# Selecting the 32nd maximum from the larger and the smaller ones of column pairs

## Chip, cores and metric

One core of a Trainium2 chip runs the whole program. The metric is the device time of one execution in microseconds; for the kernel before it is the median of three runs. A profile of one execution of the kernel before is used throughout.

Engines are called as in the profile: PE multiplies matrices (PEld is its loading of weights), DVE, ACT and POOL work on vectors, SP issues most DMAs.

## What is computed

Top-k attention is followed by a Fourier mixing block. The attention part has batch 8, 8 heads, 576 tokens and 64 channels a head:

```python
scores = scale * np.matmul(q, k.transpose(0, 1, 3, 2))
kth = np.partition(scores, -top_k, axis=-1)[..., -top_k:-top_k + 1]   # top_k = 32
mask = scores >= kth
scores = np.where(mask, scores, -1000000000.0)
scores = scores - np.max(scores, axis=-1, keepdims=True)
attn = np.exp(scores)
attn = attn / (np.sum(attn, axis=-1, keepdims=True) + 1e-09)
return np.matmul(attn, v).astype(np.float32)
```

So each of the 8 x 8 x 576 rows of 576 scores needs its largest and its 32nd largest value. The heads are then joined to x of 576 x 512 per batch, and the second block takes the real part of a two-dimensional Fourier transform over tokens and channels, adds x, normalises each row, and applies a two-layer network (512 to 2048 to 512, with a ReLU between) whose output is added again.

## The kernel before, in words

**Items and steps.** Two heads of a batch form a pair; there are 32 pairs, four to a batch. Each pair gives nine items of 128 rows by 576 scores (the ninth joins the tails of both heads), 288 items in all. The main loop (lines 1542 to 1684) makes one step per item, and in step i it works on several items at once: PE makes the scores of item i+3, DVE selects in items i and i+1, ACT and POOL mask item i-1, ACT takes its exponential, and items further back are transposed and multiplied with v.

**Selection.** `top_ops` (line 428) makes DVE's instructions for one item. There are four rounds. In each, a MAX8 (line 446) finds the eight largest values of each row into eight columns of the tile m, and except in the last a MATCH_REPLACE8 (line 448) copies the row to the work tile wk with those eight replaced by a very small number. The profile shows a MATCH_REPLACE8 as two instructions, a MATCH_VALUE_LOAD of the eight values and the pass itself. All seven passes run over 576 columns. Rounds 0 and 1 of item i+1 and rounds 2 and 3 of item i are issued alternately in one step (lines 1657 to 1663), so that neighbours on DVE do not depend on each other; the plan's "shift" operation, if the step has one, comes behind the last of item i.

**After the selection.** `bounds` (line 451) is a POOL instruction (line 455, tile nt) that multiplies columns 0 and 31 of m, the largest and the 32nd largest value, by constants from cc. `mask` (line 466) has ACT write 0 or a very large number to wk (line 469), and POOL subtract that from the scores (line 472). `expo` (line 476) is ACT's exponential with the sum of the row (line 480). For most pairs `plane` (line 487) splits the result into two planes of 16 bits (line 493), SP writes them to memory (line 506), and `turn` (line 515) brings them back transposed; `attend` (line 576) multiplies with v on PE.

**What runs beside it.** In batch 0, the first 36 steps, no network work is ready yet, and the weights are prepared instead: each of 32 pieces takes a shift on DVE (line 217) and two operations on POOL (lines 236 and 238), with ACT conversions between. POOL also subtracts column means from the first weights (line 1410). From batch 1 on, PE does the network of the batch before (lines 1024, 1051, 1218) in between. Units of it are handed to steps by an estimate of PE's time (`fixed_cost`, `level` and the "room" of a step); those estimates are constants written in the code and know nothing of DVE or POOL. POOL adds up folds of the Fourier transform (lines 684, 695, 760; DVE does them for the first and last batch) and sums for the network (lines 1164, 1191).

**Order.** The order on each engine is that in which the code issues. Within a step, POOL's queue has the mask of the item before, planned operations ("pool0"), `some_sums`, `bounds`, more sums, then the rest of the plan. SP's queue has the DMAs in the same order.

**Buffers.** The tile m has five buffers of 32 columns; the scores S six; the work tiles W three for pairs of items and one for the joined tails.

Of the kernel before, what the change touches and what calls it, by code (L numbers as in the profile page):

```python
# [9 lines left out]
F32 = mybir.dt.float32  # L10
I32 = mybir.dt.int32
# [3 lines left out]
ALU = mybir.AluOpType  # L15

TOPK = 32
NEG = -3.4028234e38
FAR = 2.0 ** 100
P = 128  # L20
# [66 lines left out]
def kernel(  # L87
# [7 lines left out]
    out: bass.AP,  # L95
):
    nc = tc.nc
    B, H, S, D = q.shape
    DM = H * D
    DF = moe_w_ch1.shape[1]  # L100
    scale = 1.0 / float(D) ** 0.5
    HS = S // 2
# [18 lines left out]
    fs_np, fd_np, sg_np, turn_np, rows_np = _tables(S, DM)  # L121
    fs_d = nc.inline_tensor(fs_np, name="c_fs")
    fd_d = nc.inline_tensor(fd_np, name="c_fd")
    sg_d = nc.inline_tensor(sg_np, name="c_sg")
    turn_d = nc.inline_tensor(turn_np, name="c_turn")
    rows_d = nc.inline_tensor(rows_np, name="c_rows")
# [4 lines left out]
    small = ctx.enter_context(tc.tile_pool(name="small", bufs=4))  # L131
# [30 lines left out]
    cc = const.tile([P, 2], F32, name="cc", tag="cc")  # L162
# [80 lines left out]
    nat, qT_of, kT_of, v_of, PT, Ssb, Wk, Wp, M8, Nt = ({} for _ in range(10))  # L243
# [109 lines left out]
    N = len(items)  # L353
# [71 lines left out]
            nc.scalar.copy(out=s_t[r, keys], in_=sp[r])  # L425
        return 1.04

    def top_ops(i, rounds):

        if not 0 <= i < N:  # L430
            return []
# [12 lines left out]
        for r in rounds:  # L444
            src, m8 = s if r == 0 else w, m[:, 8 * r:8 * r + 8]
            ops.append(lambda src=src, m8=m8: nc.vector.max(out=m8, in_=src))  # L446
            if r < TOPK // 8 - 1:
                ops.append(lambda src=src, m8=m8: nc.vector.match_replace(w, m8, src, NEG))  # L448
        return ops

    def bounds(i):

        if i < N:
            Nt[i] = small.tile([P, 2], F32, name=f"nt_{i}", tag="nt", bufs=6)
            nc.gpsimd.tensor_tensor(  # L455
                out=Nt[i], in0=M8.pop(i)[:, 0:TOPK:TOPK - 1], in1=cc, op=ALU.mult
            )

    def pair_by_dma(pair):

        return NPB <= pair < NPAIR - 1 and pair != 2 * NPB - 1
# [860 lines left out]

    ctx.enter_context(tc.manual_schedule())
    nc.vector.memset(cc[:, 0:1], -1.0)

    warm = small.tile([P, 1], F32, name="warm", tag="rd", bufs=6)
    kn0 = batp.tile([P, NC, 2, D], F32, name="kn0", tag="y")
# [113 lines left out]
    for b in range(B):  # L1441
        end = PER_BATCH * (b + 1) - 1
        last = b == B - 1
        first, soon = b == 0, b == 1
# [28 lines left out]
        for n, t in enumerate((0, 1, 4)):  # L1473
            s = fc + (0 if quick else n // 2)
            at(s, "pe2", lambda b=b, t=t, q=quick: dft_channels(b, t, q), 1.75)
        for n, t in enumerate((0, 1, 4, 3, 2)):
            s = fc + (n // 3 if last else 0 if first else (0, 0, 1, 1, 2)[n])
# [58 lines left out]
            got += one_unit()  # L1536
        return got

    for op in top_ops(0, (0, 1)):
        op()  # L1540
    i, carry = 0, 0.0
    while i < N + 5 or plan or queue or sums:
# [53 lines left out]
        if short:  # L1596
            fixed += tok
            pair, r = divmod(i - 1, PER_PAIR)
# [12 lines left out]
        cost, got = carry, 0.0  # L1611
# [36 lines left out]
        if i < N:  # L1648
# [72 lines left out]
```

## Time and profile before

| what | value |
|---|---|
| three runs | 1788.68, 1789.32, 1792.17 us |
| median | 1789.32 us |
| profiled execution | 1791.8 us |
| its span, first to last instruction | 1790.0 us |
| mean granted PE clock | 0.961 |
| busy PE / DVE / ACT / POOL | 1641.4 / 1538.2 / 1277.7 / 927.3 us |
| MAX8, 1152 instructions | 743 to 747 ns each |
| MATCH_REPLACE8, 864 instructions | 740 ns each |
| POOL's mask subtraction (line 472), 288 | 1415 ns each |
| POOL's bounds (line 455), 288 | 204 ns each |

An engine's busy time counts its own instructions, so an engine that is busy nearly all of a stretch sets that stretch's length unless another one is just as full. Which one it is changes over the run, so the stages have to be read apart. Instructions of one engine overlap a little at their ends; the distance from one start to the next tells what an instruction costs its engine.

### The profile page before, as it was taken

How to read it: one execution, taken by the hardware profiler on the slowest of the kernel's cores; microseconds unless marked ns; L12 is line 12 of the kernel's file. 1: busy time of each engine (PE TensorE's matmuls, PEld its weight loads, DVE VectorE, ACT ScalarE, POOL GpSimd, SP SyncE). 2: the span in 40 equal slices, each digit the busy share in tenths (PEclk: the TensorE clock that was granted, in tenths of full speed). 3: DMA queues.
4: the chain of work that ended last, by engine and by line, in shares of the span. 5: the costliest groups of instructions: out<-in, count | busy, mean ns of one | idle time of the engine just before them, and what ended most of it. 6: DMA issues, size and time to landing. Idle time of an engine off the chain costs nothing.

```text
span 1790.0 us, 26146 instructions
## 1 busy us (share of the span) xinstructions
PE 1641.4 (92%) x7782; PEld 1036.8 (58%) x7782; DVE 1538.2 (86%) x3284; ACT 1277.7 (71%) x3132; POOL 927.3 (52%) x1284
## 2 busy tenths in 40 slices
PE   5666688999889999999999999999999999999998
PEld 3444455455455654557555765566565755576677
DVE  7999989998899999999999999999999999861110
ACT  6878748777788778877787778877887778652200
POOL 4768845655644565355553665356535555343122
PEclk7877799999999999999999999999999999999999
DMA  5333115751457855577556865596557755630051
GB/s 155 114 102 114 34 34 149 214 155 44 121 132 199 214 145 131 141 210 193 129 148 179 222 138 138 148 240 151 141 139 212 189 134 140 169 90 13 6 180 59
DMA packets 486589, 248.97 MB, mean 139 GB/s; under 512 B 364336, under 2 KB 476720, under 8 KB 486448
## 3 DMA queue, kind: packets, MB, share of 16 engines
q1 hardware_dynamic: 482672, 237.51, 50.6%
q0 software_dynamic: 2816, 9.44, 1.5%
q8 instruction: 62, 1.02, 0.2%
q14 instruction: 79, 0.65, 0.1%
q10 hardware_dynamic: 960, 0.36, 0.1%
HBM read 93.49 MB, written 84.74 MB: 100 GB/s over the span
## 4 chain that ended last, share of the span: by engine, by line
PE 52%; DVE 14%; ACT 14%; POOL 13%; issue 5%; DMA 2%; SPq 1%; POOLq 0%; DVEq 0%
PE hp L1024 19%; DVE m L446 6%; PE o L585 6%; DVE wk L448 6%; POOL wk L472 4%; PE cp L1051 4%; PE cw L1218 4%; PE cv L1218 4%; PE sp L422 4%; ACT wk L469 3%; POOL fold L695 3%; PE cp L1089 2%; ACT wk L493 2%; ACT S L480 2%; PE yp L782 2%
## 5 line engine op out<-in xcount | busy, mean ns | idle before, releaser
L472 POOL TENSOR_TENSOR wk<-S,wk 128x576 f32<-128x576 f32 x288 | 407.6, 1415 | 445.1 <-ACT wk L469 437.7
L446 DVE MAX8 m<-wk 128x8 f32<-128x576 f32 x864 | 618.8, 743 | 0.1
L1024 PE MATMUL hp<-unT,w 128*128 128x256 f32 (+1 forms) x2048 | 527.3, 408 | 8.2 <-ACT hT L1028 6.8
L1024 PEld LDWEIGHTS hp<-unT,w 128*128 128x128 f32 x2048 | 378.0, 191 | 112.0 <-ACT hT L1028 11.7
L448 DVE MATCH_REPLACE8 wk<-m,wk 128x576 f32<-128x576 f32 x576 | 426.3, 740 | 0.0
L469 ACT ACTIVATE wk<-S,nt 128x576 f32<-128x576 f32 x288 | 224.4, 779 | 93.5 <-POOL nt L455 93.0
L493 ACT COPY wk<-S 128x576 uint16<-128x576 uint16 x468 | 290.5, 674 | 0.0
L1051 PE MATMUL cp<-w,hT 128*128 128x512 f32 x512 | 236.3, 600 | 0.0
L446 DVE MAX8 m<-S 128x8 f32<-128x576 f32 x288 | 215.1, 747 | 12.5 <-ACT S L396 12.3
L480 ACT ACTIVATE S<-wk,nt 128x576 f32<-128x576 f32 x234 | 185.1, 791 | 46.6 <-POOL wk L472 45.3
L585 PE MATMUL o<-PT,v 128*64 128x256 f32 (+3 forms) x1440 | 199.5, 422 | 15.4 <-ACT x L648 5.2
L448 DVE MATCH_REPLACE8 wk<-m,S 128x576 f32<-128x576 f32 x288 | 213.2, 740 | 0.0
L1028 ACT ACTIVATE hT<-hp 128x320 f32<-128x320 f32 (+1 forms) x256 | 104.0, 414 | 152.3 <-PE hp L1024 150.1
L422 PE MATMUL sp<-kT,qT 64*128 64x512 f32 (+1 forms) x528 | 163.8, 665 | 10.2 <-ACT means L1414 5.7
L585 PEld LDWEIGHTS o<-PT,v 128*64 128x64 f32 x1440 | 115.6, 155 | 94.3 <-issue 26.5
L425 ACT COPY S<-sp 128x512 f32<-128x512 f32 (+1 forms) x264 | 142.1, 589 | 30.3 <-PE sp L422 29.7
L1051 PEld LDWEIGHTS cp<-w,hT 128*128 128x128 f32 x512 | 93.4, 194 | 88.1 <-issue 86.9
L455 POOL TENSOR_TENSOR nt<-m,cc 128x2 f32<-128x2 f32 x288 | 58.9, 204 | 155.0 <-DVE m L446 151.7
L1164 POOL TENSOR_TENSOR hT<-hT 128x512 f32<-128x512 f32 x64 | 81.2, 1274 | 78.3 <-ACT hT L1028 55.0
L1218 PE MATMUL cw<-w,hT 128*128 128x256 f32 x448 | 106.1, 387 | 8.2 <-ACT ct L1189 4.2
L392 PEld LDWEIGHTS sp_t<-kt,qT 128*128 128x128 f32 x320 | 51.3, 194 | 104.2 <-issue 72.6
L1218 PEld LDWEIGHTS cw<-w,hT 128*128 128x128 f32 x448 | 84.1, 193 | 24.2 <-ACT ct L1189 6.2
(151 smaller groups left out, 2039.8 us busy)
## 6 DMA issues: line engine op xcount, KB each, us to landing
planes<-wk SPq DMA_DIRECT2D x208, 288.0 KB, 2.7
w<-w_parts SPq DMA_DIRECT2D x82, 512.0 KB, 5.3
space<-in_moe_w_ch_dram SPq DMA_DIRECT2D x32, 512.0 KB, 3.4
nat<-in_q_dram SPq DMA_DIRECT2D x128, 64.0 KB, 2.3
v<-in_v_dram SPq DMA_DIRECT2D x32, 256.0 KB, 3.2
nat<-in_k_dram SPq DMA_DIRECT2D x62, 128.0 KB, 3.4
planes<-wk SPq DMA_DIRECT2D x52, 144.0 KB, 2.6
w_parts<-w_t POOLq DMA_DIRECT2D x8, 512.0 KB, 4.2
```

The lines of the kernel that those rows point to most:

```text
L422: nc.tensor.matmul(sp[r], lhsT=qT[hd, q_cols], rhs=kT[hd, :], start=True, stop=True)
L425: nc.scalar.copy(out=s_t[r, keys], in_=sp[r])
L446: ops.append(lambda src=src, m8=m8: nc.vector.max(out=m8, in_=src))
L448: ops.append(lambda src=src, m8=m8: nc.vector.match_replace(w, m8, src, NEG))
L469: nc.scalar.activation(out=w, in_=Ssb[i], func=AF.Relu, scale=-FAR, bias=Nt[i][:, 1:2])
L472: nc.gpsimd.tensor_tensor(out=w, in0=Ssb[i], in1=w, op=ALU.subtract)
L480: nc.scalar.activation(out=Ssb[i] if by_dma(i) else w, in_=w, func=AF.Exp, bias=Nt.pop(i)[:, 0:1], accum_out=den_t[pair % 3][:, c:c + 1],)
L493: nc.scalar.copy(out=words[:, half, :], in_=src[:, half, :])
L585: nc.tensor.matmul(o[D * e:D * (e + 1), c0:c1], lhsT=vv[:, e, c, :], rhs=pt[:, NF if c == NF else (NF + 1) * e + c, c0:c1], start=(c == 0) ...
L1024: nc.tensor.matmul(hp[:, 0:w], lhsT=w1[:, dt, P * it:P * (it + 1)], rhs=unT[:, dt, 0:w], start=(dt == 0), stop=(dt == NDT - 1),)
L1051: nc.tensor.matmul(cp, lhsT=hT[:, it, P * n:P * (n + 1)], rhs=w2[:, it, :], start=(it == 0), stop=(it == NIT - 1),)
L1218: nc.tensor.matmul(dst, lhsT=h()[a][:, kc, :], rhs=rhs_of(kc), start=start and kc == 0, stop=kc == NK - 1, skip_group_check=True,)
```

## The change

The 576 columns of an item are taken as 288 pairs: column c and column c + 288. DVE writes the larger one of each pair to the first half of the work tile ("won") and the smaller one to the second half ("lost"). The four rounds of MAX8 and the three of MATCH_REPLACE8 then run over the 288 larger ones and give their 32 largest. One MAX8 over the 288 smaller ones gives their eight largest. A scan over eight columns, `meet`, joins the two ordered lists: its state starts with the 32nd winner and becomes, in turn, the minimum of the next higher winner and the maximum of the state and the next loser. Its last value is the 32nd largest of all 576, as long as no more than eight losers belong there.

That condition is checked. After the bounds of each item, a second POOL instruction keeps, in one column `beaten`, the largest difference so far between the 8th loser and the 24th winner. After the last item DVE turns it into ones and zeros, PE counts the rows over which it is positive, DVE writes the count as an integer, and at the end of the program every engine reads it. If it is above zero, the whole program runs once more with the selection as before. The body is therefore a function `forward` that is built twice, the second time inside a condition.

In a step the split for the larger ones comes first for item i+1; the split for the smaller ones comes behind the first MAX8 of item i's second part, the MAX8 of the smaller ones before the last MAX8, and `meet` behind it. The tile m has 48 columns and three buffers, not 32 and five, and `bounds` takes columns 0 and 47.

```diff
+    beaten = pool.tile([P, 1], F32, name="beaten", tag="beaten")
+    again = pool.tile([1, 1], I32, name="again", tag="again")
+    args = (tc, q, k, v, moe_w_ch1, moe_w_ch2, out, tables, beaten, again)
+    forward(*args, True)
+    rows = nc.values_load(again, min_val=0, max_val=P)
+    with tc.If(rows > 0):
+        forward(*args, False)
...
-            M8[i] = small.tile([P, TOPK], F32, name=f"m8_{i}", tag="m8", bufs=5)
-        w, m, s = Wk[i], M8[i], Ssb[i]
-        ops = []
-        for r in rounds:
-            src, m8 = s if r == 0 else w, m[:, 8 * r:8 * r + 8]
-            ops.append(lambda src=src, m8=m8: nc.vector.max(out=m8, in_=src))
-            if r < TOPK // 8 - 1:
-                ops.append(lambda src=src, m8=m8: nc.vector.match_replace(w, m8, src, NEG))
+            M8[i] = small.tile([P, KTH + 1], F32, name=f"m8_{i}", tag="m8", bufs=3)
+        return Wk[i], M8[i], Ssb[i]
...
+    LOST, MET, KTH = TOPK, TOPK + 8, TOPK + 15
...
+        w, m, s = work(i)
+        won, lost = (w[:, 0:HS], w[:, HS:S]) if in_pairs else (w, None)
+
+        def split(to, op):
+            return lambda: nc.vector.tensor_tensor(
+                out=to, in0=s[:, 0:HS], in1=s[:, HS:S], op=op
+            )
+
+        def best(r):
+            src = won if r or in_pairs else s
+            return lambda: nc.vector.max(out=m[:, 8 * r:8 * r + 8], in_=src)
+
+        def strike(r):
+            src = won if r or in_pairs else s
+            return lambda: nc.vector.match_replace(won, m[:, 8 * r:8 * r + 8], src, NEG)
+
+        def meet():
+
+            nc.vector.tensor_tensor_scan(
+                out=m[:, MET:MET + 8], data0=m[:, LOST:LOST + 8],
+                data1=m[:, TOPK - 2:TOPK - 10:-1], initial=m[:, TOPK - 1:TOPK],
+                op0=ALU.max, op1=ALU.min,
+            )
+
+        if part == 0:
+            ops = [split(won, ALU.max)] if in_pairs else []
+            return ops + [best(0), strike(0), best(1), strike(1)]
+        ops = [best(2), strike(2), best(3)]
+        if in_pairs:
+            ops[1:1] = [split(lost, ALU.min)]
+            ops[3:3] = [lambda: nc.vector.max(out=m[:, LOST:LOST + 8], in_=lost)]
+            ops.append(meet)
         return ops
...
+            last = KTH if in_pairs else TOPK - 1
+            m = M8.pop(i)
             nc.gpsimd.tensor_tensor(
-                out=Nt[i], in0=M8.pop(i)[:, 0:TOPK:TOPK - 1], in1=cc, op=ALU.mult
-            )
+                out=Nt[i], in0=m[:, 0:last + 1:last], in1=cc, op=ALU.mult
+            )
+            if in_pairs:
+                nc.gpsimd.tensor_scalar(
+                    out=beaten, in0=m[:, LOST + 7:LOST + 8],
+                    scalar1=m[:, TOPK - 9:TOPK - 8], scalar2=beaten,
+                    op0=ALU.subtract, op1=ALU.max,
+                )
...
+    def count_rows():
+
+        got = bank([1, 1], "rows")
+        nc.tensor.matmul(got, lhsT=beaten, rhs=cc[:, 0:1], start=True, stop=True)
+        nc.vector.tensor_scalar(
+            out=again, in0=got, scalar1=-1.0, scalar2=None, op0=ALU.mult
+        )
+        return 0.2
+
+    if in_pairs:
+        at(N + 1, "dve", lambda: nc.vector.tensor_scalar(
+            out=beaten, in0=beaten, scalar1=0.0, scalar2=None, op0=ALU.is_gt
+        ))
+        at(N + 4, "pe", count_rows)
...
-        first, second = top_ops(i, (2, 3)), top_ops(i + 1, (0, 1))
+        first, second = top_ops(i, 1), top_ops(i + 1, 0)
```

More of the change, by code (lines that the diff above doesn't have):

```diff
@@ L97, with forward @@
     nc = tc.nc
+    S, DM = q.shape[2], q.shape[1] * q.shape[3]
+    tables = tuple(
+        nc.inline_tensor(t, name=n)
+        for t, n in zip(_tables(S, DM), ("c_fs", "c_fd", "c_sg", "c_turn", "c_rows"))
+    )
+    pool = ctx.enter_context(tc.tile_pool(name="found", bufs=1))
+    beaten = pool.tile([P, 1], F32, name="beaten", tag="beaten")
[5 more added lines that the diff above has]
+        forward(*args, False)
+@with_exitstack
+def forward(
+    ctx, tc, q, k, v, moe_w_ch1, moe_w_ch2, out, tables, beaten, again, in_pairs
+):
+    nc = tc.nc
+    fs_d, fd_d, sg_d, turn_d, rows_d = tables
     B, H, S, D = q.shape
@@ L119 @@
     ROWS = {0: P, 1: P, 2: P, 3: P, 4: TAIL}
[L121 to L126, printed above, removed]
     const = ctx.enter_context(tc.tile_pool(name="const", bufs=1))
@@ L426, in scores, with work @@
         return 1.04
-    def top_ops(i, rounds):
-        if not 0 <= i < N:
-            return []
+    def work(i):
         if i not in Wk:
@@ L440, in top_ops @@
             Wk[i] = Wp[i - 1][:, 1, :] if e == 1 else Wp[i][:, 0, :]
-            M8[i] = small.tile([P, TOPK], F32, name=f"m8_{i}", tag="m8", bufs=5)
-        w, m, s = Wk[i], M8[i], Ssb[i]
-        ops = []
-        for r in rounds:
-            src, m8 = s if r == 0 else w, m[:, 8 * r:8 * r + 8]
-            ops.append(lambda src=src, m8=m8: nc.vector.max(out=m8, in_=src))
-            if r < TOPK // 8 - 1:
-                ops.append(lambda src=src, m8=m8: nc.vector.match_replace(w, m8, src, NEG))
+            M8[i] = small.tile([P, KTH + 1], F32, name=f"m8_{i}", tag="m8", bufs=3)
+        return Wk[i], M8[i], Ssb[i]
+    LOST, MET, KTH = TOPK, TOPK + 8, TOPK + 15
+    def top_ops(i, part):
+        if not 0 <= i < N:
+            return []
+        w, m, s = work(i)
[24 more added lines that the diff above has]
+            ops.append(meet)
         return ops
@@ L1324 @@
     nc.vector.memset(cc[:, 0:1], -1.0)
+    if in_pairs:
+        nc.vector.memset(beaten, -1.0)
     warm = small.tile([P, 1], F32, name="warm", tag="rd", bufs=6)
@@ L1537, in some @@
         return got
-    for op in top_ops(0, (0, 1)):
+    def count_rows():
[5 more added lines that the diff above has]
+        return 0.2
+    if in_pairs:
+        at(N + 1, "dve", lambda: nc.vector.tensor_scalar(
+            out=beaten, in0=beaten, scalar1=0.0, scalar2=None, op0=ALU.is_gt
+        ))
+        at(N + 4, "pe", count_rows)
+    for op in top_ops(0, 0):
         op()
```

## The prediction, made before the change was built

> **What bounds the kernel now.** I read the page's busy table and slices first. PE is busy 92% of the span, DVE 86%; DVE shows 9 in nearly every slice up to the 35th, PE only from the eighth. So two engines are near full, in different stretches. I then asked for the busy time of each engine in six stretches cut where that picture changes (columns: stretch, length, busy us of PE, PEld, DVE, ACT, POOL, granted clock, DMA share, GB/s):
>
> ```profile
> 0.00:230.00 230.00, 147.70 (x726) 90.33 (x727) 216.58 (x454) 179.87 (x420) 164.40 (x177) 0.78 0.33 101
> 230.00:315.00 85.00, 76.61 (x345) 47.03 (x344) 78.15 (x173) 59.56 (x154) 37.24 (x56) 0.94 0.38 97
> 315.00:540.00 225.00, 201.85 (x919) 115.71 (x918) 204.32 (x434) 172.24 (x439) 125.90 (x187) 0.95 0.50 135
> 540.00:765.00 225.00, 212.53 (x1002) 131.52 (x1000) 219.75 (x469) 179.84 (x439) 114.15 (x165) 0.98 0.64 165
> 765.00:1575.00 810.00, 794.31 (x3846) 497.89 (x3847) 766.18 (x1639) 638.07 (x1553) 429.94 (x623) 1.00 0.65 168
> 1575.00:1790.00 215.00, 208.41 (x952) 154.30 (x949) 53.23 (x120) 48.15 (x129) 55.63 (x80) 1.00 0.20 65
> ```
>
> The first 230 us (batch 0, about 38 items) belong to DVE: 94% busy with PE at 64%, and the chain of waits there gives 41% to lines 446 and 448. From 540 to 765 DVE (98%) leads, PE loses 12.5 us. From 765 to 1575 PE is at 98%: 150 items, 5.4 us each, and only 16 us of PE are idle. The last 215 us are PE alone. A faster selection can win much only at the start; later it is capped by PE's idle time, 23 + 12.5 + 16 us.
>
> Next, the costs: the groups of instructions, and the DVE timeline of one plain step.
>
> ```profile
> L446 DVE MAX8 m<-wk 128x8 f32<-128x576 f32 x864 | 618.8, 743 | 0.1
> L448 DVE MATCH_REPLACE8 wk<-m,wk 128x576 f32<-128x576 f32 x576 | 426.3, 740 | 0.0
> ```
> ```profile
> 67.51 0.40 DVE L217 TENSOR_SCALAR w<-w 128x512 int32<-128x512 int32 x1
> 67.84 0.07 DVE L448 MATCH_VALUE_LOAD wk<-m,wk 128x8 f32 x1
> 67.91 0.73 DVE L448 MATCH_REPLACE8 wk<-m,wk 128x576 f32<-128x576 f32 x1
> 68.57 0.74 DVE L446 MAX8 m<-S 128x8 f32<-128x576 f32 x1
> 69.23 0.73 DVE L446 MAX8 m<-wk 128x8 f32<-128x576 f32 x1
> ...
> 72.67 0.40 DVE L217 TENSOR_SCALAR w<-w 128x512 int32<-128x512 int32 x1
> ```
>
> Durations overlap; what counts is the distance of starts. A MAX8 or a MATCH_REPLACE8 takes 0.66 us of the engine, a MATCH_VALUE_LOAD 0.065. An item costs 7 x 0.663 + 3 x 0.065 = 4.84 us; with the shift (0.33) that makes 5.17, and the step above is 72.67 - 67.51 = 5.16.
>
> **The selection after the change.** No row has MAX8 on 288 columns. TENSOR_TENSOR rows give the rate: 128x256 takes 427 ns and 128x510 690, so 1.035 ns a column. Taking 288 columns (0.298) off leaves 0.365 us. The bounds are 0.33 (half of 0.663) and 0.66 (no gain); I take 0.365, as the fixed part must stay. Five MAX8 and three MATCH_REPLACE8: 8 x 0.365 = 2.92. Three loads: 0.20. The two splits are TENSOR_TENSORs of 288 columns; line 684 starts 0.34 us apart at 256 columns, so 0.373 each, 0.75. The scan of 8 has no row: below it lies the 0.06 us of a MATCH_VALUE_LOAD, above it the 0.42 of a 256-column op; I take 0.25, a RECIPROCAL of six columns (0.18) and 0.07 for waiting on the MAX8 right ahead. Sum 4.12: **0.72 us less per item** if nothing interferes.
>
> **What interferes.** The splits read two operands from SBUF, and POOL is busy half of the time. DVE hardly does such ops now, but where it does, batch 0's folds, this is the timeline of both engines:
>
> ```profile
> 227.64 0.43 DVE L684 TENSOR_TENSOR near<-x 128x256 f32<-128x256 f32 x1
> 227.69 0.82 POOL L695 TENSOR_TENSOR ftail<-fold 64x63 f32<-64x63 f32 x2
> 227.98 2.33 DVE L684 TENSOR_TENSOR far<-x 128x256 f32<-128x256 f32 x1
> 228.46 0.18 POOL L698 COPY ftail<-fold 64x1 f32<-64x1 f32 x1
> 228.58 0.09 POOL L725 MEMSET ftail<- 64x1 f32 x1
> 228.64 1.40 POOL L472 TENSOR_TENSOR wk<-S,wk 128x576 f32<-128x576 f32 x1
> ```
>
> The same op takes 0.43 and then 2.33 us, ending 0.27 after POOL's mask subtraction. The other such op (at 1639.8) took 1.49 and ended 0.28 after POOL's; line 217, one input, spreads from 397 to 1494 ns in the same way. So a split that finds POOL at work waits for POOL's op and then needs some 0.15 us less than its full time. How long is that wait? At a random moment the rest of POOL's running op is on average the sum of d x d / 2 over its ops, divided by the stretch. A weight step of batch 0 (5.42 us) has ops of 1.29, 1.42 and 1.34 us: 5.48 / 2 / 5.42 = 0.5; over all POOL ops of the timeline I count 0.45 for 0:230, 0.28 for 540:765, 0.29 for 765:1575. Less 0.15 in the share of moments when POOL works (0.71 and 0.5), a split pays 0.35 in batch 0 and 0.21 later. Two splits: 0.70 and 0.42. The bounds are nothing (always between POOL's ops) and 1.9 each (the row above). **The net gain per item is then 0.0 in batch 0 and 0.3 later.**
>
> The Trainium skill (SBUF — State Buffer, "Who interferes with whom") says that a DVE instruction with two SBUF inputs contends with a GpSimd instruction that reads SBUF, and that the second to issue blocks until the first is done. By that rule one op is waited for at most, up to 1.27 us for a split beside the mask; the 2.33 row let several ops of POOL pass, so it is worse than the rule.
>
> **POOL** gets 288 more ops of one column (line 455's two-column rows: 0.20 us; bounds 0.18 and 0.39) and is itself held by splits. In a plain weight step it idles 0.87 us of 5.16, which covers 0.2 + 0.5. Where batch 0's 16 mean subtractions (line 1410, 1.28 us) are added nothing covers it: 16 x 0.4 = 6 us. The op stands behind line 455 and before the mask subtraction, which waits some 1.5 us for ACT (437.7 us over 288), so it delays nothing else there.
>
> **Buffers of m** go from 5 to 3: the first MAX8 of item i+1 now waits for POOL's bounds of i-2. In the timeline these would be late in 12 steps, 19 us together, all after 315 where POOL's folds make it lag up to 11 us. PE leads there, so I count 3 us; bounds 0 and 19. The split writes the work tile 1.3 us earlier than the first MATCH_REPLACE8 did; DVE waits for copies out of that tile 4.7 us in all now, so nothing, or some 3 us if that grows. Nt's operand now waits for the scan, but the following MATCH_REPLACE8 no longer lies behind it: nothing.
>
> **The end.** Matmul and two DVE ops of the count lie beside the last batch's 180 us of PE: nothing (0.5 if not). The read of the count on every engine and the jump come after the last store. No row has either; below 0.02 us (a semaphore event), above 15 (about four round trips). I take two round trips at the 3.96 us of the first load from memory: 8 us. The Trainium skill (Runtime: NRT & Kernel Launch, "Instruction fetch mechanics") says that a jump outside the fetched window stalls on a fetch, with no figure; no run here shows it. Its 200 ns a register for a load would leave, as an estimate, a smaller part for the reading.
>
> **The sum**, against the profiled execution (1791.8 us, span 1790.0 and 1.8 around it): batch 0, selection 0 and POOL +6; 230 to 315, two engines even: +1; 315 to 540, DVE not first: -3; 540 to 765, 41 items x 0.3 = 12 against 12.5 of idle PE, half of it: -6; 765 to 1575, PE's waits name ACT, issue and POOL, hardly DVE: -3; buffers +3; end +8. Together +6, so 1798. That execution lies 2.5 us above the median of 1789.32; against the median **1795 us**, 0.3% slower.
>
> **Rivals.** *The splits slip between POOL's ops* (0.1 us of wait a step). For it: after the scan POOL waits for ACT, and the last line 472 began 1 to 3 us after line 455. Against it: batch 0's POOL ops are back to back. Batch 0's step falls from 5.42 to about 4.95, where POOL's run of 4.75 holds it: 38 x 0.47 = -18; later stages -5, -11, -6; buffers +2, end +8: -30, **1759**.
> *Waits for POOL make DVE the bound everywhere*, the other side. DVE has 44 us idle over 150 items, 0.29 each, so it decides from 0.72 + 0.29 = 1.0 us of waiting per item; the 2.33 row speaks for it, the mean of 0.42 against. At 1.2 us: 191 items x 0.2 = 38, batch 0 38 x 0.48 = 18, end 8: +64, **1853**.
> *The check fails and the second pass runs*: twice the time, 3580. From the reference's inputs, over all rows and both column orders, the 8th largest loser stays at least 0.0019 below the 24th winner, and no row has over 6 losers among its 32; float error is far smaller.
>
> **Chances.** Forecast 0.46 (1782 to 1812), slipping between 0.33, waits as bound 0.17, an end over 15 us 0.03, second pass 0.01. A measurement tells 0.2% (3.6 us). Faster: 0.33 + 0.03 of the forecast = 0.36. Same: 0.16, all of the forecast. Slower: 0.27 + 0.17 + 0.04 = 0.48. The range leaves out the far ends of both rivals: 1756 to 1832; the forecast's own is 1782 to 1812.
>
> **What would show it.** MAX8 at about 445 ns and MATCH_REPLACE8 at 440; splits of 460 ns at best with a long tail to 1.5 and more, their mean near 0.7 in the first 230 us and 0.65 later; MAX8 with idle time put down to POOL's line for the check op in few steps; the span's end some 8 us after the last store's issue. I am wrong if the splits' mean stays near 0.46 (faster), if it passes 1.0 (slower), or if batch 0 ends well before 220 us.

## The result, and the profile after

The kernel after takes **1819.53 us** (median of four executions, 1815.89 to 1824.36), the kernel before beside it 1789.61 us. The ratio is 1.0167, with an interval of 1.0136 to 1.0197: slower by 30 us. The profiled execution of after takes 1822.5 us, its span is 1820.7 us; before's span was 1790.0, so 30.7 us have to be found.

The same six stretches as before (columns: stretch, length, busy us of PE, PEld, DVE, ACT, POOL, granted clock, DMA share, GB/s), after; 30.7 us of its span lie behind the last of them:

```profile
0.00:230.00 230.00, 145.03 (x692) 88.85 (x693) 216.40 (x595) 176.69 (x410) 180.74 (x196) 0.76 0.33 101
230.00:315.00 85.00, 72.56 (x352) 45.26 (x352) 76.50 (x217) 58.17 (x152) 48.10 (x81) 0.97 0.33 80
315.00:540.00 225.00, 199.05 (x895) 112.79 (x892) 194.83 (x597) 169.88 (x434) 150.79 (x227) 0.96 0.51 135
540.00:765.00 225.00, 210.65 (x1003) 129.20 (x1002) 203.16 (x627) 178.46 (x436) 138.69 (x208) 0.97 0.62 162
765.00:1575.00 810.00, 786.99 (x3775) 489.51 (x3775) 724.78 (x2214) 630.37 (x1538) 509.57 (x761) 1.00 0.63 163
1575.00:1790.00 215.00, 210.17 (x973) 152.79 (x971) 66.63 (x186) 65.04 (x167) 63.51 (x95) 1.00 0.27 81
```

From 765 to 1575, DVE is busy 41 us less than before (724.78 for 766.18), and PE is busy less too (786.99 for 794.31). So an engine got relief and the other did less work in the same time. POOL is busier in every stretch. This is not the picture of a DVE that has become the bound, nor of a gain that was capped.

The groups of instructions of after, by line (line numbers are always those of the kernel shown):

```profile
L474 DVE MAX8 m<-wk 128x8 f32<-128x288 f32 x1152 | 493.0, 446 | 36.1 <-POOL beaten L508 35.7
L468 DVE TENSOR_TENSOR wk<-S 128x288 f32<-128x288 f32 x576 | 358.2, 622 | 30.0 <-DMA planes<-wk 18.4
L478 DVE MATCH_REPLACE8 wk<-m,wk 128x288 f32<-128x288 f32 x864 | 375.4, 438 | 0.0
L482 DVE TENSOR_TENSOR_SCAN m<-m 128x8 f32<-128x8 f32 x288 | 127.2, 442 | 10.1
L508 POOL TENSOR_SCALAR beaten<-m,beaten 128x1 f32<-128x1 f32 x288 | 115.8, 402 | 0.0
```

The second number behind the bar is the mean of one in ns. The passes shrank as forecast. The means of the split (622) and of the scan (442) say little by themselves; the views of the two lines by themselves give shortest, middle and longest:

```profile
L468 DVE TENSOR_TENSOR wk<-S x576: 395/443/5993, 10.9 to 1630.3; 128x288 f32<-128x288 f32 x192
L482 DVE TENSOR_TENSOR_SCAN m<-m x288: 232/235/2160, 17.2 to 1631.9; 128x8 f32<-128x8 f32 x144
```

Half of the scans take at most 235 ns, but the mean is 442: the scan is held like the splits. How, the timeline of a weight step shows, DVE and POOL together:

```profile
62.36 0.81 DVE L474 MAX8 m<-wk 128x8 f32<-128x288 f32 x2
62.64 1.28 POOL L250 TENSOR_TENSOR w<-w,space 128x512 int32<-128x512 int32 x1
63.09 1.15 DVE L468 TENSOR_TENSOR wk<-S 128x288 f32<-128x288 f32 x1
63.88 1.63 POOL L527 TENSOR_TENSOR wk<-S,wk 128x576 f32<-128x576 f32 x1
```
```profile
71.22 1.29 POOL L252 TENSOR_TENSOR w<-w,space 128x512 f32<-128x512 f32 x1
71.30 0.45 DVE L474 MAX8 m<-wk 128x8 f32<-128x288 f32 x1
71.78 0.76 DVE L482 TENSOR_TENSOR_SCAN m<-m 128x8 f32<-128x8 f32 x1
72.47 0.41 DVE L231 TENSOR_SCALAR w<-w 128x512 int32<-128x512 int32 x1
```

The split ends at 64.24, 0.32 us after POOL's line 250 (63.92). The scan ends at 72.54, just after POOL's line 252 (72.51). In the first piece POOL's mask subtraction, which begins while the split still runs, takes 1.63 us; its mean before was 1.415 and is 1.465 now. So the holding goes both ways.

**Where the time came from.** The start of POOL's bounds of an item marks when its 32nd maximum is in use. From the timelines, in us, items counted from 0:

| bounds of item | before | after | difference |
|---|---|---|---|
| 36 (first behind batch 0) | 222.9 | 229.7 | +6.8 |
| 144 | 823.0 | 836.7 | +13.7 |
| 279 | 1558.2 | 1585.5 | +27.3 |
| 287 (last) | 1611.6 | 1639.1 | +27.5 |
| span's end | 1790.0 | 1820.7 | +30.7 |

The loss grows over the whole run, also where DVE has work to spare. Behind the last item only 3.2 us come on top.

How it reaches PE shows between the bounds of items 144 and 279, where PE runs 3489 instructions in both kernels. That stretch takes 735.2 us before and 748.8 after; PE is idle 11.7 and 21.3 us of it. ACT waits 49.5 us there for the bounds before, 61.1 after, and what PE waits for more are other results of ACT, the copies of the scores first of all (before, then after; us in total, times, longest):

```profile
PE tpq L329 <- ACT S L396: 1.7, 3, 0.6
```
```profile
PE tpq L343 <- ACT S L410: 7.1, 5, 2.2
```

PE's wait for ACT's hidden layer (hp <- ACT hT) goes from 2.1 to 4.4 us. ACT takes its work in the order of the code, so a wait for the bounds delays the copies behind it; that this is the way of the delay is read from these waits, not tested.

### The profile page after: what moved, and what is told of

Same layout as the page of the kernel before. It is cut to its first block, busy times and chain, and to the rows that moved or that the text cites. A ratio compares the mean times of both kernels' runs of the same rounds, so it can differ in the third digit from the quotient of the medians.

```text
span 1820.7 us, 27785 instructions
## 1 busy us (share of the span) xinstructions
PE 1647.6 (90%) x7784; PEld 1037.8 (57%) x7784; DVE 1486.0 (82%) x4439; ACT 1278.6 (70%) x3132; POOL 1100.1 (60%) x1572
## 4 chain that ended last, share of the span: by engine, by line
PE 51%; ACT 15%; POOL 13%; DVE 13%; issue 4%; DMA 3%; SPq 1%; POOLq 0%; DVEq 0%
PE hp L1079 19%; PE o L640 5%; PE cw L1273 5%; POOL wk L527 5%; PE cv L1273 4%; PE sp L436 4%; DVE wk L468 3%; PE cp L1106 3%; PE cp L1144 3%; ACT wk L524 3%; DVE m L474 3%; DVE wk L478 3%; POOL fold L750 3%; ACT wk L548 2%; ACT S L535 2%
## 5 line engine op out<-in xcount | busy, mean ns | idle before, releaser
L527 POOL TENSOR_TENSOR wk<-S,wk 128x576 f32<-128x576 f32 x288 | 422.0, 1465 | 361.7 <-ACT wk L524 361.0
L1079 PE MATMUL hp<-unT,w 128*128 128x256 f32 (+1 forms) x2048 | 526.6, 408 | 13.4 <-ACT hT L1083 11.7
L474 DVE MAX8 m<-wk 128x8 f32<-128x288 f32 x1152 | 493.0, 446 | 36.1 <-POOL beaten L508 35.7
L468 DVE TENSOR_TENSOR wk<-S 128x288 f32<-128x288 f32 x576 | 358.2, 622 | 30.0 <-DMA planes<-wk 18.4
L478 DVE MATCH_REPLACE8 wk<-m,wk 128x288 f32<-128x288 f32 x864 | 375.4, 438 | 0.0
L524 ACT ACTIVATE wk<-S,nt 128x576 f32<-128x576 f32 x288 | 224.2, 779 | 108.7 <-POOL nt L504 108.3
L439 ACT COPY S<-sp 128x512 f32<-128x512 f32 (+1 forms) x264 | 142.0, 588 | 27.3 <-PE sp L436 26.7
L504 POOL TENSOR_TENSOR nt<-m,cc 128x2 f32<-128x2 f32 x288 | 79.0, 274 | 120.3 <-DVE m L482 111.0
L482 DVE TENSOR_TENSOR_SCAN m<-m 128x8 f32<-128x8 f32 x288 | 127.2, 442 | 10.1
L494 DVE MAX8 m<-wk 128x8 f32<-128x288 f32 x288 | 126.1, 438 | 0.0
L508 POOL TENSOR_SCALAR beaten<-m,beaten 128x1 f32<-128x1 f32 x288 | 115.8, 402 | 0.0
```

Of the source, the lines that this page charges most:

```text
L468: return lambda: nc.vector.tensor_tensor(out=to, in0=s[:, 0:HS], in1=s[:, HS:S], op=op)
L474: return lambda: nc.vector.max(out=m[:, 8 * r:8 * r + 8], in_=src)
L478: return lambda: nc.vector.match_replace(won, m[:, 8 * r:8 * r + 8], src, NEG)
L524: nc.scalar.activation(out=w, in_=Ssb[i], func=AF.Relu, scale=-FAR, bias=Nt[i][:, 1:2])
L527: nc.gpsimd.tensor_tensor(out=w, in0=Ssb[i], in1=w, op=ALU.subtract)
L1079: nc.tensor.matmul(hp[:, 0:w], lhsT=w1[:, dt, P * it:P * (it + 1)], rhs=unT[:, dt, 0:w], start=(dt == 0), stop=(dt == NDT - 1),)
```

## The experiments

The theories, which each expectation states again in its own words: **C**, the held splits (and what they hold on POOL) make results late; **D**, the result comes later in the step because the scan stands last, whoever is held; and smaller ones: **A**, the check loads POOL; **B**, three buffers of m tie DVE to POOL; and the end. "Late" below is measured at the bounds, as in the table above.

### The check op left out (e1_no_check)

The maximum over the differences is never formed, so the second pass could not be called for.

```diff
-            if in_pairs:
-                nc.gpsimd.tensor_scalar(
-                    out=beaten, in0=m[:, LOST + 7:LOST + 8],
-                    scalar1=m[:, TOPK - 9:TOPK - 8], scalar2=beaten,
-                    op0=ALU.subtract, op1=ALU.max,
-                )
```

> The POOL instruction that compares the 8th loser with the 24th winner of every item is left out (the count of failing rows stays at none, and the second pass stays behind its condition). Theory A, the check loads POOL and makes it late in its heavy steps: POOL's busy time falls by about 116 us to 985, DVE's wait for m shrinks, and the time falls by 14 to 22 us to 1798 to 1806. Theory B, three buffers of m tie DVE to POOL whatever POOL does: the buffer is freed 0.4 us earlier per item, DVE's 36 us of waiting falls to about 25, the time by 3 to 6 us. Theory C, waits of the two-operand DVE instructions for POOL: unchanged but for the collisions with the check itself, 0 to 5 us.

Measured: 1812.53 us, ratio 1.0129 (1.0109 to 1.0149). That is 7 us less than after, more than B's 3 to 6 and C's 0 to 5 and less than A's 14 to 22, with intervals that overlap a little (after's begins at 1.0136). POOL's busy time falls from 1100.1 to 985.7 us, the splits' mean only from 622 to 598. The check is a small part; over 20 us remain without it.

### Five buffers of m (e2_five_bufs)

The losers' eight columns are written into columns that are free again, so that m fits into 32 columns.

```diff
-            M8[i] = small.tile([P, KTH + 1], F32, name=f"m8_{i}", tag="m8", bufs=3)
+            M8[i] = small.tile([P, TOPK], F32, name=f"m8_{i}", tag="m8", bufs=5)
...
-                out=m[:, MET:MET + 8], data0=m[:, LOST:LOST + 8],
+                out=m[:, TOPK - 1:TOPK - 9:-1], data0=m[:, LOST:LOST + 8],
```

> m is packed into 32 columns (losers take the place of the second eight winners, the scan writes over the last eight) and gets five buffers as before the change; all instructions stay. Theory B: DVE's 36 us of waiting for the check to free m goes to under 3 us and the time falls by 8 to 18 us to 1802 to 1812. Theory A: DVE no longer waits, but POOL's bounds and mask come as late as before, PE's idle time stays, and the time stays within 4 us of 1819.5. Theory C: the same as A.

Measured: 1819.79 us, ratio 1.0162 (1.0140 to 1.0185), the same as after. The wait itself is gone, as the groups of this kernel show beside the 35.7 us above; in the scan's line the mean is now 517 instead of 442:

```profile
L478 DVE MAX8 m<-wk 128x8 f32<-128x288 f32 x1152 | 490.1, 445 | 0.2
L487 DVE TENSOR_TENSOR_SCAN m<-m 128x8 f32<-128x8 f32 x288 | 148.9, 517 | 10.1
```

A wait of 36 us in the profile was worth nothing: DVE's idle time falls by 21 us only, and its busy time rises by 20 (1506.2 for 1486.0), in scans that are held longer.

### The second pass left out (e3_no_second)

The count is formed but not read, and the body is built once.

```diff
-    rows = nc.values_load(again, min_val=0, max_val=P)
-    with tc.If(rows > 0):
-        forward(*args, False)
```

> The read of the count and the second pass are left out; the check of every row and the count stay. All theories: the steps do not change. The span ends about 3 us after the last store's issue, as before the change, and not 5.8 us after it: 2 to 4 us less. If holding a second program mattered beyond the end (loading of code, for example), the steps would get shorter too, and the time would fall by more than 5 us.

Measured, a single execution: 1822.49 us, span 1820.6. The total does not tell it apart, the end does. SP's last issue in before (span 1790.0), after (1820.7) and this kernel (1820.6), from the three timelines:

```profile
1787.10 0.34 SPq L997 DMA_DIRECT2D out_dram<-x  x1
```
```profile
1814.94 0.34 SPq L1052 DMA_DIRECT2D out_dram<-x  x1
```
```profile
1817.66 0.34 SPq L1049 DMA_DIRECT2D out_dram<-x  x1
```

From there to the span's end it is 2.9 us before, 5.8 after and 2.9 without the read and the jump. **Reading the count and passing over the second body cost 2.9 us.**

### The splits as reductions over one operand (e4_reduce)

```diff
-            return lambda: nc.vector.tensor_tensor(
-                out=to, in0=s[:, 0:HS], in1=s[:, HS:S], op=op
+            return lambda: nc.vector.tensor_reduce(
+                out=to, in_=s.rearrange("p (h c) -> p c h", h=2), op=op,
+                axis=mybir.AxisListType.X,
```

> Both splits are made by a reduction over the pair, an instruction with one operand of 576 elements, so that DVE reads no second operand there. Theory C, the collisions on both sides are what costs: a split takes about 0.74 us with no spread instead of a mean of 0.62, POOL's mask subtraction goes back from 1465 to about 1415 ns, and the time falls by 5 to 15 us. Theories A and B: DVE pays 2 x 0.12 us more per item and gains nothing on POOL; batch 0 gets longer by 5 to 9 us and the time rises by 3 to 12 us.

Measured: 1804.26 us, ratio 1.0077 (1.0058 to 1.0097). The line of the splits in this kernel:

```profile
L468 DVE TENSOR_REDUCE wk<-S x576: 695/749/783, 10.8 to 1613.8; 128x288 f32<-128x576 f32 x192
```

A reduction is dearer than a split on the mean (748 ns for 622), and DVE's busy time *rises* from 1486.0 to 1541.9 us; the kernel is 15 us faster all the same. What has gone is the spread: no split is longer than 783 ns. POOL's operations are shorter too: the mask subtraction falls from 1465 to 1415 ns, the bounds from 274 to 202. So the mean of a held operation is the wrong price for it here; whether the holds on DVE or those on POOL cost more, this run does not separate.

### The second part first in the step (e5_meet_early)

After, but in each step item i's part goes ahead of item i+1's, so that the scan is not the last.

```diff
+        order = [(first, 0), (second, 0), (first, 1), (second, 1), (first, 2), (first, 3),
+                 (second, 2), (first, 4), (second, 3), (first, 5), (second, 4)]
```

> The changed kernel with another order within the step: item i's second part runs ahead of item i+1's first part, so that the scan has the last MATCH_REPLACE8 of item i+1 behind it and no longer ends the step. Theory D, the 32nd maximum comes too late in the step, ACT (in order) waits for the bounds and PE for what stands behind on ACT: ACT's 108 us of waiting for nt falls below 95 and the time falls by 5 to 12 us to 1808 to 1815. Theory C, only the number and length of the collisions count: within 4 us of 1819.5.

Measured: 1827.75 us, ratio 1.0224 (1.0200 to 1.0248): slower still. The splits now meet POOL more (mean 670 ns for 622), and ACT waits 116.5 us for the bounds instead of 108.3. Theory D (1808 to 1815) is not borne out, and C's "within 4 us" is missed as well; but two things changed at once. The same order is tried again below without held splits.

### Before, with the last MAX8 at the end of the step (e6_before_late)

```diff
+        order = [(second, 0), (first, 0), (second, 1), (first, 1), (second, 2), (second, 3), (first, 2)]
```

> The kernel before the change with one exchange in the order: the last MAX8 of item i is issued behind the last MATCH_REPLACE8 of item i+1, so that its result ends the step, as the scan does after the change; every instruction keeps its length. Theory D: ACT's wait for nt rises from 93 to over 100 us and the time rises by 4 to 12 us to 1793 to 1801. Otherwise: within 3 us of 1789.

Measured: 1801.87 us, ratio 1.0074 (1.0053 to 1.0094). DVE's instructions are the same, nothing in the selection reads two operands, and the time rises by 13 us, just above D's 1793 to 1801; ACT's wait for the bounds rises from 93.0 to 117.0 us. But the exchange also put a MAX8 right ahead of the MATCH_VALUE_LOAD that reads its result, which before keeps apart:

```profile
960.67 0.74 DVE L446 MAX8 m<-wk 128x8 f32<-128x576 f32 x1
961.44 0.09 DVE L448 MATCH_VALUE_LOAD wk<-m,wk 128x8 f32 x1
```

From the start of the MAX8 to the load it is 0.77 us here; the middle of all such pairs is 775 ns, for 659 before. DVE's busy time rises by 24 us (1562.5 for 1538.2), and it idles 10 us more ahead of the loads that work on wk. So lateness and 34 us more of DVE changed together, and that a late result costs by itself is not shown.

### Before, with a check op on POOL (e7_before_check)

```diff
+            nc.gpsimd.tensor_scalar(
+                out=beaten, in0=m[:, TOPK - 1:TOPK], scalar1=m[:, TOPK - 9:TOPK - 8],
+                scalar2=beaten, op0=ALU.subtract, op1=ALU.max,
```

Its result is not used.

> The kernel before the change with the POOL check added for every item (32nd against 24th value, so that it has the same form and length) and nothing done with it. Theory A, POOL's load alone makes time: 288 x 0.36 = 104 us more of POOL, 5 to 12 us more in all, 1794 to 1801. If POOL has room for it when nothing else holds it: 0 to 3 us more, and the 7 us that leaving the check out of the changed kernel gave come only together with the collisions.

Measured: 1790.11 us, ratio 1.0001 (0.9990 to 1.0012). The op takes 365 ns on the mean, nearly twice the 0.20 us that was forecast, and costs nothing that can be measured in a kernel without the splits and the scan. So the 7 us of the first experiment are not its length alone; that they need the held splits and scans beside it fits, but is argued.

### One last round over all 576 columns (e8_one_last_round)

Rounds 0 to 2 run over the larger ones; the fourth MAX8 runs over what is left of both halves and gives the 32nd maximum directly. No losers' MAX8, no scan; the splits are reductions, the check (the same kind of difference) is a DVE operation one step later, m has 32 columns and five buffers, and item i's part goes first.

```diff
-            src = won if r or in_pairs else s
+            src = w if r == 3 else won if r or in_pairs else s
...
-            ops[3:3] = [lambda: nc.vector.max(out=m[:, LOST:LOST + 8], in_=lost)]
-            ops.append(meet)
```

> A version made from what the runs showed. The fourth round is one MAX8 over all 576 columns, the struck larger ones and the smaller ones together: its eight values are the 25th to the 32nd as long as at most eight smaller ones exceed the 24th larger one. The scan, the MAX8 of the smaller ones and the extra columns of m go, m has 32 columns and five buffers, the splits are reductions with one operand, the check (32nd above 24th) is a DVE instruction one step later, and item i goes first in the step. DVE per item: 6 x 0.365 + 0.663 + 0.20 + 2 x 0.67 + 0.1 = 4.5 us against 4.84 before the change, with no two-operand DVE instruction, so POOL back to about 927 us. Theory C (collisions): batch 0 gains 0.3 us an item, 11 us, later stages up to 10, the end costs 3: 1768 to 1784. If the loss came from the doubled program or its end, it stays above 1790.

Measured: 1790.22 us, ratio 1.0008 (0.9998 to 1.0018): no difference from before. DVE's busy time is 47 us below before's (1491.1 for 1538.2), and the last bounds come 5.2 us earlier; the end takes 2.9 of them. Theory C's 1768 to 1784 is missed: 47 us less of DVE brought 5.2. The order of this version, too, puts a MAX8 right ahead of the load of its result.

### The splits as reductions, and the second part first (f1_reduce_early)

The order of e5_meet_early in the kernel e4_reduce.

> The changed kernel with both splits as reductions over one operand (1804.3 us when run alone) and, besides, the second part of item i issued ahead of the first part of item i+1 in each step, so that the 32nd maximum is ready before the step's end. Theory D (what the change still costs without the held splits is that the result comes later than before and ACT and PE start later): ACT's wait for the bounds falls from what it was with the reductions towards the 93 us of the kernel before, and the time falls by 5 to 10, to 1794 to 1799. Theory S (only DVE's own sum and its meetings with POOL count, the place in the step does not): 1801 to 1808.

Measured: 1796.43 us, ratio 1.0056 (1.0034 to 1.0077). The median and ACT's wait for the bounds (93.2 us for 108.2) are where D wants them; the interval overlaps that of e4_reduce (1.0058 to 1.0097), so it is not settled by this pair alone. The scans are held as before (mean 444 ns for 421, the longest 6147), so what a held scan costs hangs on the order around it. And the scan no longer stands right behind the MAX8 whose result it reads: from the start of the MAX8 ahead to the scan it is 359 ns, for 486 in e4_reduce (middle values), so lateness is again not the only difference.

### The scan as a MAX8 over sixteen columns (f2_max_meet)

The eighth of the last eight winners and the eight losers together is the 32nd maximum under the same condition. The splits are reductions, so no operation of the selection reads two operands now; the order, the check on POOL, the three buffers and the second pass are after's.

```diff
-            nc.vector.tensor_tensor_scan(
-                out=m[:, MET:MET + 8], data0=m[:, LOST:LOST + 8],
-                data1=m[:, TOPK - 2:TOPK - 10:-1], initial=m[:, TOPK - 1:TOPK],
-                op0=ALU.max, op1=ALU.min,
-            )
+            nc.vector.max(out=m[:, MET:MET + 8], in_=m[:, TOPK - 8:TOPK + 8])
```

> The changed kernel with the splits as reductions and the scan of eight columns replaced by one MAX8 over sixteen columns (the last eight winners and the eight losers), which reads one operand; its eighth value is the 32nd maximum. No DVE instruction of the selection reads two operands any more. Theory M (the scan's waits for POOL, 421 ns on the mean where it has 232 at best, delay the result): the MAX8 takes 150 to 250 ns with no spread and the time falls by 4 to 10, to 1794 to 1800. Rival: DVE's time isn't what the end waits for, so the 0.2 us an item change nothing: 1801 to 1808.

Measured: **1789.40 us**, ratio 1.0006 (0.9996 to 1.0016), 15 us below e4_reduce: M's direction, and more than the 4 to 10 it had given. The mean falls from 421 to 178 ns, 187 of it the hold and 56 the shorter free time; the new operation stands in the scan's place and starts 486 ns after the start of the MAX8 ahead, as the scan did. The line of the new operation, and the long stretch of this kernel:

```profile
L483 DVE MAX8 m<-m x288: 177/178/180, 17.7 to 1600.0; 128x8 f32<-128x16 f32 x144
```
```profile
765.00:1575.00 810.00, 794.61 (x3849) 500.01 (x3847) 736.91 (x2227) 635.10 (x1547) 481.69 (x771) 1.00 0.66 169
```

All 288 take 177 to 180 ns. PE is back at 794.61 us of 810 (before 794.31), while DVE, at 736.91, has 29 us less to do than before. The last bounds come at 1606.0, 5.5 us earlier than before; the rest of the run is 3.2 us longer. The second body is in this program too, and the time is that of before, so carrying it costs little beyond the end.

### The last-round kernel with its splits of two operands (f3_last_round_split)

```diff
-            return lambda: nc.vector.tensor_reduce(
-                out=to, in_=s.rearrange("p (h c) -> p c h", h=2), op=op,
-                axis=mybir.AxisListType.X,
+            return lambda: nc.vector.tensor_tensor(
+                out=to, in0=s[:, 0:HS], in1=s[:, HS:S], op=op
```

> The version with one last round over all 576 columns (1790.2 us, splits as reductions) with its two splits as instructions of two operands again. Theory C (the splits held by POOL cost the time that was found between the changed kernel and its form with reductions, 15 us): 1798 to 1810, the splits' mean near 0.6 us and a last bounds 8 to 20 us later. Rival (only the sum of DVE's busy time counts): two splits of 0.6 instead of 0.75 make DVE's sum smaller by 0.3 us an item, so 1785 to 1791.

Measured: 1805.22 us, ratio 1.0106 (1.0077 to 1.0135), 15 us more than e8_one_last_round with 61 us *less* DVE time. The splits' groups in the two kernels, this one first:

```profile
L468 DVE TENSOR_TENSOR wk<-S 128x288 f32<-128x288 f32 x576 | 337.2, 625 | 48.7 <-ACT S L410 19.8 <-ACT wk L518 14.7 <-DMA planes<-wk 13.7
```
```profile
L468 DVE TENSOR_REDUCE wk<-S 128x288 f32<-128x576 f32 x576 | 409.1, 752 | 27.2 <-ACT S L410 9.4 <-ACT wk L519 8.5 <-DMA planes<-wk 8.3
```

Theory C holds in both directions: taken out of after, 15 us less; put into a kernel without it, 15 us more. A sum of DVE's time has the wrong sign both times.

### The last-round kernel in after's order (f4_last_round_late)

The order list of e8_one_last_round is taken out again.

> The version with one last round over all 576 columns (1790.2 us) with the step's order of the changed kernel: the first part of item i+1 goes ahead, and the last MAX8 of item i is the step's last selection instruction. DVE's work is the same to the instruction. Theory D (lateness of the result costs by itself): 1795 to 1803, ACT's wait for the bounds up from 80.9 us by 10 to 30. Rival (place in the step doesn't matter): 1788 to 1793.

Measured: 1787.28 us, ratio 0.9990 (0.9975 to 1.0004): not slower. ACT waits 83.0 us for the bounds, 80.9 with the other order. D's 1795 to 1803 is missed. But this was no clean test of it: the last MAX8 of item i has the last MATCH_REPLACE8 of item i+1 behind it in this order too, so its result does not end the step, and no MAX8 stands right ahead of the load of its result any more, which takes 24 us off DVE's busy time (1467.4 for 1491.1) and 10 off its idle time ahead of the loads. In all three of e6_before_late, f1_reduce_early and this run the time went the way of DVE's waits for its own last result; lateness by itself was never changed alone. It is also the lowest time of all, but not told apart from before.

### What the holds cost, step by step

Two kernels that differ in the held operations and in what stands in for them can be laid beside each other at the bounds of each item. For each step from the bounds of one item to the next (items 1 to 278), I added up by how much its splits and scans exceed their middle durations in after (443 and 235 ns), and took how much longer that step is than in the other kernel:

| held in the step | after beside f2_max_meet | f3_last_round_split beside e8_one_last_round |
|---|---|---|
| under 0.4 us | 134 steps, -1.1 us | 188 steps, -9.7 us |
| 0.4 to 0.8 us | 47 steps, +6.5 us | 28 steps, +4.0 us |
| over 0.8 us | 97 steps, +29.5 us | 62 steps, +20.4 us |
| all | +34.9 us | +14.7 us |

A step with a long hold is 0.3 us longer; the others don't win back what DVE saved, or only a part. For the scan alone (e4_reduce beside f2_max_meet) the loss stands one step later: the 32 steps that *follow* a hold of over 0.8 us are 15.5 us longer, all the other steps together are even (-0.4). This is a comparison of two profiled executions each, so an argument beside the experiments; its totals are near theirs (34.9 us beside 30.1, 14.7 beside 15.0).

## Why the forecast was right, and where it was not

The direction was right and the wide range, 1756 to 1832, held the time. That was in part luck: the forecast's own range, 1782 to 1812, did not, and the wide one only reached so far because it took in the near side of the rival at 1853. The size was 24.5 us short (1795 for 1819.5), and the way there was another.

**The operations themselves: right.** MAX8 446 ns and MATCH_REPLACE8 438 (forecast 445 and 440); a free split 443 (460); the splits' means 823 ns up to 230 us and 579 to 684 in the later stretches, 591 over all of them (0.7 and 0.65). So a split waits 0.38 in batch 0 and 0.15 later, for 0.35 and 0.21 forecast. The estimate from POOL's running operations was good for the mean, not for the shape: 28% of the splits took 480 ns or more, 0.64 us over the middle on the mean, where POOL works in 50 to 71% of moments.

**The scan: mis-sized.** Forecast 0.25, of which 0.07 for waiting on the MAX8 right ahead, with an upper bound of 0.42; its mean duration is 0.44, and the wait on that MAX8 is 0.12 (481 ns from the MAX8's start to the scan, where 360 is usual). The step that failed: "The splits read two operands" was applied to two operations, and the third that reads two operands, the scan, was priced by its width. The Trainium skill (SBUF — State Buffer, "Who interferes with whom") speaks of any DVE instruction with two SBUF inputs, and so would have named the scan; the rows here agree (235 ns free, 2160 at the longest). By f2_max_meet the scan, as it stands at the end of the step, is 15 us; f1_reduce_early, with scans held as much, lies 7 above f2_max_meet, so the 15 are not a fixed price of the hold.

**"The net gain per item is then 0.0 in batch 0 and 0.3 later": the step that failed.** As a sum it was not far off: DVE's busy time fell by 52 us, 0.18 an item. But the terms made from it, +1 - 3 - 6 - 3 for 230 to 1575, came out as some +21 (27.5 - 6.8, buffers in it). I had netted the holds against the shorter passes. The runs show that they don't net: a saved 0.3 us in a step where PE leads is worth next to nothing (PE at 98%, which the prediction itself used as a cap; 47 us less of DVE brought 5.2 in e8_one_last_round), while a step with over 0.8 us of hold is 0.3 us longer. e4_reduce and f3_last_round_split show it for the splits: more DVE time and faster, less DVE time and slower. The prediction had also read PE's waits as naming "hardly DVE" and so gave later stages only gains; the delay reaches PE under ACT's name.

**POOL and the check: number right by luck, reason wrong.** The op took 402 ns, not 0.20 (bound 0.39). Batch 0 lost 6.8 us where +6 was forecast. But e7_before_check loses nothing with this op, and in f2_max_meet, which has it, the bounds of item 36 come at 221.6, before the 222.9 of before. The loss in batch 0 is not the check's length either: most of it goes when the splits stop being held (224.0 in e4_reduce) as well as when the check goes (225.0 in e1_no_check). That POOL is held as well was mentioned, and charged in 16 steps of batch 0 only: its busy time rose by 173 us, of which the check is 116 and the longer bounds and mask 35 (20 and 14).

**Buffers: +3 forecast, none found.** The wait was there, 35.7 us in 23 waits for 19 in 12 forecast, and e2_five_bufs took it away for nothing.

**The end: +8 forecast, 2.9 measured.** One round trip of the 3.96 us row would have been nearer than two. The Trainium skill (Runtime: NRT & Kernel Launch, "Instruction fetch mechanics") lets a far jump wait for a fetch; whatever of that there is lies within these 2.9 us, together with the reading.

**The rivals.** The other side came true, but not by its mechanism: "waits for POOL make DVE the bound everywhere" needed 1.0 us of waiting per item, and there were 0.57 (0.36 of two splits, 0.21 of the scan); DVE was busy 725 of 810 us. Splits slipping between POOL's operations did happen (412 of 576 took under 480 ns); it did not help, since the other 164 set the loss. The second pass did not run.

So the 30 us are: 15 from the splits with two operands, 15 from the scan, shown by taking each away in turn; what is left, the end's 2.9 and the 5.5 that the last bounds come earlier, nearly cancels. What stays open is why scans that are held as much cost 15 us in after's order and about 7 in that of f1_reduce_early, and whether the holds on DVE or on POOL weigh more. The way to PE is clear in part: between items 144 and 279 PE's wait for ACT's score copies is 7.1 us in after, 3.1 in e4_reduce, and 1.7 in f2_max_meet as before. ACT's own wait for the bounds is no measure of it: over the whole run it is as long in e4_reduce (108.2) as in after (108.3), at 15 us less.

## What to carry to other kernels

Before a wide one-operand pass is replaced by several cheap operations, count which of the new ones read two operands from SBUF, the tiny ones too, and look whether POOL runs beside them: a free duration and even the mean are the wrong price, since the long tail costs and the savings in between may not count. A dearer operation without a spread can be the faster one (748 ns for 622 here). Where another engine is at 98%, as PE is here, a gain on this one may be worth nothing while a delay is not. And before two orders of the same instructions are compared, look which ones stand right behind the one whose result they read.

## What the runs showed of the hardware

- A scan over eight columns, 235 ns when free, was held for up to 2160 ns in after and 6147 in f1_reduce_early, so width was no protection. A MAX8 over sixteen columns took 177 to 180 in 288 cases.
- TENSOR_REDUCE over pairs 288 columns apart, one operand of 576, took 695 to 783 ns in 576 cases beside the same POOL work. This agrees with what the Trainium skill (SBUF — State Buffer, "Who interferes with whom") states of this operation: that it never contends on trn2.
- A held operation can let several of POOL's pass. One split of after ran beside seven, from 592.51 to 598.50, and ended 0.31 us after the last of them; that is rare, only 7 of the 164 longer splits (480 ns and up) ran beside more than two:

```profile
592.51 5.99 DVE L468 TENSOR_TENSOR wk<-S 128x288 f32<-128x288 f32 x1 [2.27 <-DMA planes<-wk]
```
```profile
592.59 1.27 POOL L1219 TENSOR_TENSOR hT<-hT 128x512 f32<-128x512 f32 x1
...
595.56 1.40 POOL L527 TENSOR_TENSOR wk<-S,wk 128x576 f32<-128x576 f32 x1
596.93 1.26 POOL L1219 TENSOR_TENSOR hT<-hT 128x512 f32<-128x512 f32 x1
```

  The first fence is DVE's timeline, the second POOL's.
- A POOL TENSOR_SCALAR of one column with two more columns as its scalars took 365 ns on the mean in the kernel without splits and scan (e7_before_check), a TENSOR_TENSOR of two columns 203 in the same kernel. Here the form counted for more than the width.
- A DVE instruction right behind the MAX8 whose result it reads starts later: a MATCH_VALUE_LOAD 775 ns after the start of a MAX8 over 576 columns (e6_before_late) instead of 659 (before), a scan 481 after the start of one over 288 columns (after) instead of 359 (f1_reduce_early).
